# A convolution and gated-MLP kernel: a written-out order of operations rearranged between its last convolution stage and its first tile pair

## The chip, the core and the metric

The kernel runs on one NeuronCore of a Trainium2 chip. The core has five engines with a queue of instructions each, which they work off in order: TensorE (PE, matmuls), VectorE (DVE), ScalarE (ACT), GpSimd (POOL) and SyncE (SP, which here only issues DMA transfers). They meet at semaphores. PE reads SBUF and writes PSUM; the other three compute from and to SBUF, and DVE and ACT also from PSUM. The metric is the time of one execution on the device in microseconds, the median over several runs.

## The reference

Two blocks act on 2048 rows of 640 numbers, both under a modulation that is computed from a vector `c`:

```
mod = silu(c) @ w_mod                      -> sa, ca, ga, sb, cb, gb
h   = layernorm(x) * (1 + ca) + sa
kv  = shortconv4(k) * v
y   = longconv(kv, ssm_k) + kv * ssm_D     (reference: FFT over 4096)
x   = x + ga * (h * y)
h   = layernorm(x) * (1 + cb) + sb
z   = gelu(h @ w_in);  z1, z2 = halves of z
g   = w_sp @ layernorm(z2) + b_sp          (2048 x 2048 over the rows)
out = x + gb * ((z1 * g) @ w_out)
```

The long convolution is done by matrix products with trigonometric tables. The product with `w_sp` is the largest: for each pair of row tiles it takes seven block products (a Strassen-like scheme) instead of eight.

## The kernel before

The rows are 16 tiles of 128, handled in four groups of four tiles (`TB = 4`); the 640 columns are five units `u` of 128 (`NU = 5`). A first part does the convolution unit by unit; a second turns the result `xt` into `z` group by group; the third, a loop over pairs of tiles (p, p + 8) from line 1147, does the seven products and the projection with `w_out`.

The first two parts, and the first tile pair of the third, are not emitted in the order of the source. Each step is recorded with `op(...)` (line 97) as an entry of a plan: the engines that may run it, its function and what it reads and writes. The string `ORDER` (line 40) then lists all 1086 entries in the order of emission, each with the letter of the engine that runs it (P, A, D, G, S for PE, ACT, DVE, POOL, SP). Since each engine works in order, this string fixes every queue; waits follow from the data and from the buffers that are used again. There is no planner at work when the kernel is built: the order is written out by hand, or by something outside the kernel. Lines 1145 on, the main loop, are outside the plan.

The steps that are touched, with their numbers in `ORDER`:

- `res` (line 698), `xt += gh`: the residual sum of one unit of the convolution, for the four tiles of one group (512 numbers per partition) or for two (256). It may stand on DVE or GpSimd, for the last unit on DVE only. G666 to G669 are unit 2, D/G692, 697 and 702 unit 3, D728, 732, 737, 744 and 751 unit 4 (the last), 610, 611 and 644 earlier units of the later groups.
- `ghm` (line 661), two products or sums on `gh` before that (711, 712, 714), and `yml` (line 746), `gh *= y` from PSUM (D727, 731, 736, 743, 750).
- `ln2` (line 704) and `ag2` (line 829): bn_stats and bn_aggr of the new `xt`, tile by tile; `rstd2` (lines 190 and 191) on GpSimd; `nmr2` (line 833) on DVE.
- `zx` (lines 843, 845, 847): the normalised tile, on ACT, GpSimd or DVE (762, 763, 775, 776 for group 0; 840 to 843 for group 1; 906 to 909; 972 to 975).
- Group 0 comes in two pieces of two tiles. They are transposed by PE (`hfl`, line 858: P764, P765 and P777, P778) and modulated from PSUM to SBUF (`hmod`, lines 871 and 869: 766 to 770, 779 to 783). Groups 1 to 3 are transposed by a DMA (`turn`, line 889: S844, S910, S976) and modulated in place (`hmod2`, lines 897 and 895: 845 to 849, 911 to 915, 977 to 981), on DVE, ACT or GpSimd.
- `zz`: five matmuls of 432 columns for half a tile of `z1` or `z2`, 16 times for each group, each followed by `gelu` on ACT (line 920). P850, P926 and P982 or P999 are the first of groups 1, 2 and 3 that touch their group.
- `stz`, `agz`, `rstdz`, `nmrz`, `zn`: the layernorm of `z2` (lines 926, 930, 190, 935, 943 and 941).
- `ssum` (line 988, D1054 to D1061), sums of tiles of `w_sp`, and `tsum` (line 998, D1062 to D1069), sums of `z2`, for the seven products; `prodw` (line 1013, P1070 to P1083).
- `gbm` (line 1077, D1046 to D1052): `w_out` times `gb`; `bcol` D1053.
- S1038 to S1043 load `w_sp` tiles with a transposing DMA, S1045 is seven transfers of `w_out`, S1044 the bias.
- `fill`: matmuls with the identity whose result nobody uses. P1036 has four, P1037 three; both write the tile tag `s1`, of which there is one buffer, and which the first of each pair of flips also uses.

The buffers that matter: `pu` and `pz` two each and `sm` two in PSUM, `s1` one; `Z` three and `X1` four in SBUF.

Of the kernel before, what the change touches and what calls it, by code (L numbers as in the profile page):

```python
# [65 lines left out]
P425 A426 D482 D663 P664 D498 S583 P517 D518 G677 G483 G484 P485 A486 P507 D508 P499 P459 A460 P469 P501 A470 D665  # L66
G675 G519 G520 P521 A522 G509 G510 A500 A132 G708 P487 P584 D502 P513 D488 P511 A512 P491 P489 G503 A490 D514 P515
G504 D492 S678 G668 P505 P679 A516 A506 G493 D494 P495 A585 D633 D680 P681 D682 A496 P719 A720 D636 S586 P683 D684
P715 P721 A722 D716 P685 D686 D687 P717 A718 P587 A588 P723 P726 P725 G711 P724 G666 D688 D689 G714 D727 D728 D730
D759 G702 D729 P735 P749 G667 D758 D731 P1037 P589 A590 D732 D734 D691 D772 G760 D761 D762 D763 P764 D750 P765 D766  # L70
D767 D768 D733 D690 D771 P742 S756 G692 D696 D736 D737 D739 D740 A769 A770 S757 P784 A785 G773 D774 P816 A817 A776
P812 D637 D695 D836 G775 A813 P794 A795 D693 D741 D738 D834 D837 D694 D835 P777 D779 D780 D781 P778 A782 G838 D839
D840 D843 A783 P787 A788 D842 G841 D751 S844 D754 D697 D712 D743 D611 D700 D744 D748 G644 P818 P824 A825 D701 A819
D699 D746 P820 A821 P814 P805 A806 G610 D641 P791 D642 G669 D643 S1045 A815 D796 S1041 P822 A792 A823 D640 D747 D902
D848 D845 D847 P808 A809 D901 G846 P801 A849 A802 D745 D698 D706 D900 P826 D648 P798 A799 P850 D903 A851 D852 P860
A827 A861 P864 A865 P884 A885 P892 D1050 G904 D905 P867 A868 D906 D907 D909 A893 P857 P890 A858 A891 S1040 P880 A881
D793 P888 A889 G908 D803 S910 D755 P878 A879 P871 D645 G911 A913 A872 S1038 P874 P886 D866 D800 A875 P853 P882 A912
# [1133 lines left out]
```

## Time and profile before

| | |
|---|---|
| median of 3 runs | 314.68 us (314.50 to 316.01) |
| profiled execution | 314.39 us, span 312.6 us |
| PE matmuls | 298.4 us busy, 95% of the span |
| DVE | 259.9 us, 83% |
| ACT | 158.0 us, 51% |
| POOL | 117.8 us, 38% |
| granted PE clock, mean | 0.989 |

The profiled execution is one run; durations of instructions come from it, and its span begins with the first instruction and ends with the last. A row of the timeline gives the start in us from the span's beginning, the duration, engine, line, operation, what it writes and reads with shapes, the count of like instructions merged, and in brackets the idle time of the engine before it with what ended that. A row of a stretch gives, for each engine, busy time and the count of instructions, then the granted clock of PE and the share and rate of the DMA engines. Matmuls are pipelined: a row is longer than the spacing of two matmuls.

### The profile page before, as it was taken

How to read it: one execution, taken by the hardware profiler on the slowest of the kernel's cores; microseconds unless marked ns; L12 is line 12 of the kernel's file. 1: busy time of each engine (PE TensorE's matmuls, PEld its weight loads, DVE VectorE, ACT ScalarE, POOL GpSimd, SP SyncE). 2: the span in 40 equal slices, each digit the busy share in tenths (PEclk: the TensorE clock that was granted, in tenths of full speed). 3: DMA queues.
4: the chain of work that ended last, by engine and by line, in shares of the span. 5: the costliest groups of instructions: out<-in, count | busy, mean ns of one | idle time of the engine just before them, and what ended most of it. 6: DMA issues, size and time to landing. Idle time of an engine off the chain costs nothing.

```text
span 312.6 us, 6393 instructions
## 1 busy us (share of the span) xinstructions
PE 298.4 (95%) x2499; PEld 198.7 (64%) x2506; DVE 259.9 (83%) x520; ACT 158.0 (51%) x284; POOL 117.8 (38%) x147
## 2 busy tenths in 40 slices
PE   7988899999999999799799999999999999999996
PEld 2665688868899988555355555555555656555564
DVE  8898998989999998999997999977676758577473
ACT  6998899988888867166366777130101010010100
POOL 2442877858987998445315712000000000000000
PEclk9999999999999999899799999999999999999999
DMA  8999999996997679005997800065958284840414
GB/s 169 231 222 232 254 288 234 216 229 158 233 208 156 134 140 361 26 2 109 212 193 123 163 2 0 1 95 101 189 76 206 62 176 104 134 101 0 103 29 114
DMA packets 127953, 45.22 MB, mean 145 GB/s; under 512 B 117071, under 2 KB 127156, under 8 KB 127924
## 3 DMA queue, kind: packets, MB, share of 16 engines
q1 hardware_dynamic: 127770, 44.78, 67.7%
q8 instruction: 19, 0.31, 0.4%
q14 instruction: 10, 0.08, 0.1%
q10 hardware_dynamic: 154, 0.05, 0.1%
HBM read 16.11 MB, written 5.24 MB: 68 GB/s over the span
## 4 chain that ended last, share of the span: by engine, by line
PE 51%; DVE 6%; POOL 0%; issue 0%
PE ps L1013 23%; PE po L1137 10%; PE pu L245 7%; PE pz L245 7%; DVE st L704 2%; PE pz L1013 2%; PE pu L1013 1%; DVE xt L698 1%; DVE Z L847 1%; DVE gh L746 1%; DVE gh L661 0%; DVE mv L829 0%; DVE Z L871 0%; POOL rstd L191 0%; PE s L245 0%
## 5 line engine op out<-in xcount | busy, mean ns | idle before, releaser
L245 PEld LDWEIGHTS <-Z 128*128 128x128 bf16 x320 | 31.8, 100 | 30.7 <-DVE Z L897 2.7
L245 PE MATMUL pu<-X,M 128*128 128x128 bf16 (+1 forms) x480 | 45.8, 237 | 2.4 <-DVE Tf L462 2.1
L245 PEld LDWEIGHTS <-M 128*128 128x128 bf16 x480 | 37.3, 98 | 8.8 <-issue 3.3
L1019 ACT COPY m<-ps 128x432 f32<-128x432 f32 x7 | 3.6, 519 | 73.8 <-PE ps L1013 73.8
L476 POOL TENSOR_TENSOR W<-Tf 128x256 bf16<-128x256 f32 x47 | 34.7, 758 | 11.3 <-DVE Tf L462 7.9
L1013 PEld LDWEIGHTS <-S 128*128 128x128 bf16 x256 | 25.0, 98 | 21.7
L245 PE MATMUL pu<-big,Z 128*128 128x432 bf16 x160 | 33.4, 357 | 2.1 <-DVE Z L897 2.1
L248 ACT CAST X<-s 128x1024 bf16<-128x1024 f32 x31 | 31.9, 1028 | 2.0 <-PE s L245 1.8
L245 PE MATMUL pz<-big,Z 128*128 128x432 bf16 x160 | 32.7, 353 | 0.0
L1137 PE MATMUL po<-w_o,uT 128*128 128x320 bf16 (+2 forms) x231 | 32.7, 295 | 0.0
L462 DVE TENSOR_TENSOR Tf<-pu,KH 128x1024 f32<-128x1024 f32 x25 | 30.3, 1219 | 2.6 <-POOL gh L608 1.1
L1013 PEld LDWEIGHTS <-wT 128*128 128x128 bf16 x192 | 18.7, 98 | 15.5 <-issue 0.3
L1137 PEld LDWEIGHTS <-uT 128*128 128x128 bf16 (+1 forms) x231 | 22.2, 97 | 9.7
L245 PEld LDWEIGHTS <-G 128*128 128x128 bf16 x330 | 24.7, 98 | 2.3 <-issue 0.5
L248 ACT CAST KH<-pu 128x512 bf16<-128x512 f32 x40 | 23.0, 600 | 5.1 <-PE pu L245 5.1
L248 ACT CAST Z<-pz 128x512 bf16<-128x512 f32 x38 | 22.3, 601 | 5.3 <-PE pz L245 5.1
L1013 PE MATMUL ps<-X,wT 128*128 128x432 bf16 x112 | 22.7, 346 | 0.1
L1013 PE MATMUL ps<-T,S 128*128 128x432 bf16 x112 | 22.7, 346 | 0.0
L1013 PE MATMUL ps<-X,S 128*128 128x432 bf16 x112 | 21.6, 346 | 0.0
L245 PEld LDWEIGHTS <-X 128*128 128x128 bf16 x288 | 18.1, 98 | 5.1 <-DMA X<-kv_scr 1.6
L245 PE MATMUL sm<-big,dg 128*128 128x512 bf16 (+3 forms) x73 | 20.0, 382 | 0.4
L245 PE MATMUL s<-F1bd,X 128*128 128x256 bf16 x128 | 19.2, 272 | 0.5 <-ACT X L248 0.2
(181 smaller groups left out, 547.0 us busy)
## 6 DMA issues: line engine op xcount, KB each, us to landing
wm<-in_w_mod_dram SPq DMA_DIRECT2D x6, 800.0 KB, 6.1
xt<-in_A_q_dram SPq DMA_DIRECT2D x4, 640.0 KB, 6.2
out_dram<-ot SPq DMA_DIRECT2D x15, 160.0 KB, 2.1
big<-in_B_w_in_dram SPq DMA_DIRECT2D x2, 1080.0 KB, 9.6
X<-in_A_ssm_k_dram SPq DMA_DIRECT2D x4, 512.0 KB, 5.2
kv_scr<-big SPq DMA_DIRECT2D x4, 512.0 KB, 3.5
X<-kv_scr SPq DMA_DIRECT2D x4, 512.0 KB, 4.7
w_o<-in_B_w_out_dram SPq DMA_DIRECT2D x6, 160.0 KB, 2.9
```

The lines of the kernel that those rows point to most:

```text
L245: nc.tensor.matmul(o, lhsT=w, rhs=x, start=start, stop=stop)
L248: (e.copy if e is nc.scalar else e.tensor_copy)(dst, src)
L462: e.tensor_tensor(T_[:], (tl[pu] if src is None else tl[src])[:, :, :, None, :].to_broadcast(shape), tl[KH][:, :, None, :, :].to_broadcast ...
L476: e.tensor_tensor(tl[W][:, :, o, :], T_[:, :, 0, o, :], T_[:, :, 1, 1 - o, :], op=ALU.add if o else ALU.subtract)
L698: op("GD" if u < NU - 1 else "D", "res", lambda e: e.tensor_tensor(sl, sl, gl, op=ALU.add), r=[("gh", (u, g))], w=[("xt", (u, n)) for n in ...
L704: op("D", "ln2", lambda e, n=n: e.bn_stats(out=st2[:, n, (0, 0, 0, 1, 2)[u], :], in_=xt[:, n, us[0] * DU:(u + 1) * DU]), r=[("xt", (v, n)) ...
L746: op("D", "yml", lambda e, ghv=ghv, py=py, i0=i0, k=k: e.tensor_tensor(ghv, ghv, tl[py][:, i0:i0 + k], op=ALU.mult), r=[py], w=[("gh", (u, ...
L847: e.tensor_scalar(dst, xt[:, n, :], mv2[:, n, 0:1], rstd2[:, n:n + 1], op0=ALU.subtract, op1=ALU.mult)
L1013: nc.tensor.matmul(ps[:, :FC], lhsT=lhs[:, s_, :], rhs=rhs(s_), start=(s_ == 0 and not more), stop=(s_ == HT - 1), skip_group_check=more)
L1019: nc.scalar.copy(part[p, m][:], part[p, BANK[m]][:, :FC])
L1137: nc.tensor.matmul(ps[:, :hi - lo], lhsT=uTs[t][:fsz[ft], ft, :], rhs=w_o[:fsz[ft], ft, lo:hi], start=(ft == 0), stop=(ft == NFT - 1))
```

## The change

Only `ORDER` changes, from its 692nd entry on: rows 69 to 87 of the file. No step is added or dropped; what changes is the sequence, and for 33 steps the engine. Up to there every queue is as it was. The entries that changed engine: 644, 697, 702, 712 (residuals and `ghm` of units 1, 3 and 4), 762, 763, 775, 776, 840, 841, 843, 972 to 974 (`zx`), 845, 846, 848, 849, 913 to 915, 977, 979, 980 (`hmod2`), 832, 896, 897, 899, 963, 964, 1028, 1029, 1031 (`zn`). GpSimd has 29 entries in this part instead of 30, DVE 187 instead of 182, ACT 82 instead of 86.

The main moves by queue. On GpSimd: G692 comes before G760 and the residuals G667, G610 and G697 between G760 and G838; 702 and 644 go to DVE, 697 and 712 to GpSimd. On DVE: D691 comes ahead of D727, D736, D750, D737 and two `ln2` ahead of D766; D1054 to D1057 move forward to behind D810; D1060, D1061 and four of the `gbm` move behind D1084. On PE: P1036 moves from the very end to behind P1037, the `zz` of each group change places, and P1016 becomes the last. On SP: S1038 and S1039 come between S844 and S910, S1040 and S1045 between S910 and S976, the rest behind.

```diff
-P715 P721 A722 D716 P685 D686 D687 P717 A718 P587 A588 P723 P726 P725 G711 P724 G666 D688 D689 G714 D727 D728 D730
-D759 G702 D729 P735 P749 G667 D758 D731 P1037 P589 A590 D732 D734 D691 D772 G760 D761 D762 D763 P764 D750 P765 D766
-D767 D768 D733 D690 D771 P742 S756 G692 D696 D736 D737 D739 D740 A769 A770 S757 P784 A785 G773 D774 P816 A817 A776
-P812 D637 D695 D836 G775 A813 P794 A795 D693 D741 D738 D834 D837 D694 D835 P777 D779 D780 D781 P778 A782 G838 D839
-D840 D843 A783 P787 A788 D842 G841 D751 S844 D754 D697 D712 D743 D611 D700 D744 D748 G644 P818 P824 A825 D701 A819
-D699 D746 P820 A821 P814 P805 A806 G610 D641 P791 D642 G669 D643 S1045 A815 D796 S1041 P822 A792 A823 D640 D747 D902
-D848 D845 D847 P808 A809 D901 G846 P801 A849 A802 D745 D698 D706 D900 P826 D648 P798 A799 P850 D903 A851 D852 P860
...
-S976 G980 P940 A979 A941 P958 A977 P930 A931 D856 G894 D1061 A959 D929 D1055 D1057 D942 D935 P944 A945 P937 D918 A938
...
-D1068 D1069 D1078 D1082 P1074 P1076 P1083 D1075 D1079 S1080 P1010 A1011 D1084 D1048 P1018 A1019 P1022 A1023 D1049
-D1052 S1085 D1051 P1036 D1047 D1046
+P715 P721 A722 D716 P685 D686 D687 P717 A718 P587 A588 P723 P726 P725 G666 D691 G711 D689 D688 P724 D727 G714 G692
+D728 D729 D758 D730 D759 G760 D690 D731 D732 D734 P735 P1037 D772 P1036 D761 A762 P749 D736 D750 D737 P589 S756 D741
+D740 G763 P764 D766 D767 D768 S757 A590 G667 G610 D696 P765 A769 P742 D733 D738 D693 D834 D771 A770 D637 P794 G773
+D695 D836 P812 P784 A795 A813 D751 D754 D774 P818 D837 P791 A775 D739 D694 D835 G697 D698 D776 P778 G838 A819 D839
+A785 A840 D842 G843 P777 A782 A783 P787 A788 P816 A817 D780 G712 D841 P814 A815 D640 A792 D779 D781 P808 A809 D796
+D752 P822 A823 S844 P820 A821 P824 A825 A846 P798 A848 D743 D789 D702 G669 D703 D706 G845 D744 D745 D746 D900 P801
+D611 A799 D644 S1038 P805 A806 D793 P826 A802 A827 D641 D699 D901 D847 G849 P850 A851 D797 P857 P867 A868 D747 P892
+A893 D643 D701 D755 D748 P882 D903 S1039 A883 D700 D642 D902 A858 P874 A875 D647 P880 G904 D905 D906 G908 D786 D907
+D909 S910 D810 A881 P890 A891 P860 G915 A861 P864 A865 G911 P871 A872 P884 D1054 D1055 D1057 D705 D968 A912 D1056 D807
+D811 G913 A885 D648 D704 D753 D645 D966 D646 D967 D969 G970 D866 P888 A889 S1040 D859 D862 D863 P886 A914 P878 A887
+A879 P853 D790 D971 D972 G975 D973 A974 A854 D855 D800 P926 P916 A927 S1045 P937 A917 D852 D869 S976 D1046 D803 D804
...
+D964 D1064 D1066 D1030 A1028 A1015 D1029 D1065 P1024 P1070 A1025 P1072 S1044 P1077 D1067 P1081 D1053 A1073 D1068 D1069
+A1071 P1074 D1078 D1082 P1076 D1075 D1079 S1080 P1083 P1018 A1019 P1022 P1010 A1023 D1084 S1085 A1011 D1060 D1061
+P1016 A1017 D1047 D1051 D1052 D1050
```

More of the change, by code (lines that the diff above doesn't have):

```diff
@@ L73 @@
-D840 D843 A783 P787 A788 D842 G841 D751 S844 D754 D697 D712 D743 D611 D700 D744 D748 G644 P818 P824 A825 D701 A819
-D699 D746 P820 A821 P814 P805 A806 G610 D641 P791 D642 G669 D643 S1045 A815 D796 S1041 P822 A792 A823 D640 D747 D902
-D848 D845 D847 P808 A809 D901 G846 P801 A849 A802 D745 D698 D706 D900 P826 D648 P798 A799 P850 D903 A851 D852 P860
-A827 A861 P864 A865 P884 A885 P892 D1050 G904 D905 P867 A868 D906 D907 D909 A893 P857 P890 A858 A891 S1040 P880 A881
-D793 P888 A889 G908 D803 S910 D755 P878 A879 P871 D645 G911 A913 A872 S1038 P874 P886 D866 D800 A875 P853 P882 A912
@@ L78 @@
-A887 A854 D705 A883 D869 D647 D968 D752 D704 D810 D753 D646 D967 D969 D703 D966 D1060 D914 D1058 G970 D971 D915 A972
-G973 D859 D804 P926 P916 A917 D1059 G975 D807 A927 D811 D789 P948 D876 S1044 D1053 P952 S1039 D1056 D928 D873 D877
-A949 P923 A924 G974 D870 P946 A947 A953 D855 P919 A920 D786 D790 D925 D797 P954 D1054 A955 D862 D863 G828 P933 A934
-S976 G980 P940 A979 A941 P958 A977 P930 A931 D856 G894 D1061 A959 D929 D1055 D1057 D942 D935 P944 A945 P937 D918 A938
-D895 D898 A899 D897 D896 G978 D921 D922 D829 D832 G981 D939 D943 P999 D932 D936 G960 P982 A1000 D830 A983 D984 S1042
@@ L83 @@
-D1001 P992 A993 P1020 A1021 D961 P989 A990 D1063 D833 P985 A986 P1006 A1007 A962 P996 A997 D965 P1003 A1004 D831 P1024
-D994 D991 D995 D987 D988 P1014 D1008 P956 D1005 D1009 A1025 A1015 P1016 D998 D1002 G1026 D963 D1062 A964 D1064 D1027
-D1030 A957 A1017 P1012 A1013 S1043 P950 A1029 A951 P1072 A1073 D1028 P1070 D1031 D1065 A1071 D1066 D1067 P1077 P1081
-D1068 D1069 D1078 D1082 P1074 P1076 P1083 D1075 D1079 S1080 P1010 A1011 D1084 D1048 P1018 A1019 P1022 A1023 D1049
-D1052 S1085 D1051 P1036 D1047 D1046
+P715 P721 A722 D716 P685 D686 D687 P717 A718 P587 A588 P723 P726 P725 G666 D691 G711 D689 D688 P724 D727 G714 G692
@@ new lines @@
+P933 D918 S1041 A934 P930 P940 A938 D1048 A941 D876 D873 D877 D870 D856 D928 A931 D932 D980 P919 D942 A920 G894 P923
+D921 A924 P948 P958 G979 P952 D895 A959 D922 A949 P946 P954 D977 A896 D925 D929 A947 A953 A955 D939 G978 G981 P982
+A983 G828 P999 D1058 D1059 A897 D898 A1000 D943 P985 A986 P989 A990 P992 D829 D830 D831 D1049 A832 D833 D935 D936
+D1001 D984 D987 A993 D988 P944 P1006 A945 A1007 P996 A997 D1062 P1003 A1004 D991 P956 G960 D961 D965 A962 A957 D1008
+D998 D1002 D1005 D1009 P1020 S1043 A1021 A963 S1042 D994 D995 D899 D1063 P1012 P1014 A1013 P950 G1026 D1027 A1031 A951
```

## The prediction

> **What bounds the kernel now.** I read the page's engine shares (PE 95%, DVE 83%), then the chain that ended last, then busy time by stretches cut at PE's gaps, then the timelines of PE, DVE and POOL around them. The chain, in order of time (start, us, what):
>
> ```profile
> 139.41 1.56 DVE Z L847 x3
> 140.97 1.30 DVE xt L698
> 142.59 0.97 DVE xt L698
> 149.93 0.68 DVE Z L897 x2
> 206.53 0.88 PE s L245 x4
> 207.45 8.92 PE ps L1013 x48
> ```
>
> Up to 150.6 the chain runs on VectorE; from 150.66 it is matmul after matmul to the end. Two VectorE handoffs and then pure PE work set the time. Stretches (PE, PEld, DVE, ACT, POOL busy, then granted clock):
>
> ```profile
> 128.27:130.47 2.20, 0.00 (x0) 0.00 (x1) 2.13 (x7) 0.43 (x1) 1.77 (x2) 1.00 0.00 0
> 130.47:134.19 3.72, 3.63 (x48) 2.59 (x49) 3.41 (x10) 1.02 (x2) 0.53 (x2) 0.54 0.02 4
> 148.60:150.66 2.06, 0.00 (x1) 0.01 (x1) 2.03 (x8) 0.53 (x1) 0.00 (x0) 1.00 0.87 255
> 150.66:155.09 4.43, 4.43 (x16) 2.00 (x16) 3.91 (x14) 1.48 (x3) 2.19 (x3) 0.61 0.98 204
> 155.09:207.45 52.36, 52.31 (x286) 27.89 (x285) 49.05 (x114) 31.45 (x57) 15.26 (x18) 1.00 0.46 82
> ```
>
> PE stands still twice, and each time runs at about half clock for 3 to 4 us afterwards. Then it has no idle left. Timelines of VectorE and GpSimd (start, us, shape, count):
>
> ```profile
> 128.06 0.29 DVE L698 TENSOR_TENSOR xt<-xt,gh 128x256 bf16<-128x256 bf16 x1
> 129.19 0.87 DVE L833 SCALAR_TENSOR_TENSOR nmr<-mv,rstd 128x2 f32<-128x2 f32 x1
> 140.89 1.36 DVE L698 TENSOR_TENSOR xt<-xt,gh 128x512 bf16<-128x512 bf16 x1
> 142.50 1.05 DVE L698 TENSOR_TENSOR xt<-xt,gh 128x512 bf16<-128x512 bf16 x1
> 145.48 0.42 DVE L698 TENSOR_TENSOR xt<-xt,gh 128x512 bf16<-128x512 bf16 x1
> ```
>
> ```profile
> 128.90 1.14 POOL L698 TENSOR_TENSOR xt<-xt,gh 128x512 bf16<-128x512 bf16 x1
> 140.76 3.80 POOL L698 TENSOR_TENSOR xt<-xt,gh 128x512 bf16<-128x512 bf16 x3
> ```
>
> The same residual takes 0.42 alone and 1.36 beside a GpSimd one; nmr2 (0.14 alone, row 135.25) takes 0.87 and ends at 130.06, with GpSimd's 130.04.
>
> **The Trainium skill.** "SBUF — State Buffer", Who interferes with whom: the port pair that VectorE and GpSimd share is an exclusive lock; a VectorE operation with two SBUF inputs, or in a two-port mode, and a GpSimd operation that reads SBUF block each other, whoever comes second. The trace agrees (0.42 against 1.36). "TensorE: Matmul & The Clock Gate", What's actually happening: the array's clock is halved after an idle window of some 3.4 us, in free-running windows. The half clock and its length agree (3.72 and 4.43 us stretches); that a whole idle window is needed does not: 2.06 us sufficed here, while 1.06 us (PE's timeline at 22.4) left the clock at 1.00.
>
> **The loss before.** Running groups overlap by 0.16 in the timeline, so the gaps cost 2.20 + 0.16 = 2.36 and 2.06 + 0.16 = 2.22. Slow clock: from 130.47 to 134.19, 10 transposes (0.055 each at full rate, from the pair at 136.93), 32 short matmuls (0.80) and 5 long ones (0.91) would take 2.26; they took 3.72: 1.46. From 150.66 to 155.09, 15 long ones at 0.182: 2.73 instead of 4.43: 1.70. Sum 7.74 us. PE's other work from 128 to the main loop is the same in both kernels, the fillers too, so what counts is how much of 7.74 remains.
>
> **The change, part by part** (letter and number are ORDER's).
>
> *Fillers P1036.* Four matmuls (0.216 apart, 0.86) leave the end, where they are on the chain, and go behind P1037. They run in the first gap. They write the one s1 buffer that P1037 writes, so a drain of about 0.2 comes in between (a row is 0.38 long, 0.216 apart). PE's last group before the gap starts at 127.43, five times 0.136 apart, so PE is free at 128.11 + 0.86 + 0.2 = 129.2.
>
> *First handoff.* One more bn_stats goes ahead of D727, which had waited for PE until 125.36: +0.1. Residual D728 now finds GpSimd free (only G692 is left there, over by 125.3): 0.29 instead of 0.90. The second ag2 then ends at 127.74 + 0.1 − 0.6 = 127.24. rstd2 takes 0.1 + 1.07 (row 127.84): 128.4. Five VectorE operations (1.62, as 127.66 to 129.28) run until 128.8, nmr2 unblocked until 128.95. The two normalisations go to ACT (0.91) and GpSimd (0.88) at once and end at 129.9; before, both stood on VectorE until 130.77 and PE started at 130.47. PE starts at 129.95: idle 0.75.
>
> *First matmuls of group 0.* Ten transposes and P742: 0.55 + 0.80, PE free at 131.3. VectorE does D736 and D750 (0.66 each, one input in PSUM: no lock) until 130.1; residual D737 then meets G667, which starts at 129.85 and takes 1.15: blocked, it ends 0.28 after it, as in the 140.89 row: 131.3. Two bn_stats (0.2 apart), then the hmods: first at 132.15, next two 0.33 apart. Idle 0.85, and 0.3 inside the first group: 1.15.
>
> *Second piece.* Five groups of 0.91 bring PE to 137.0. The flips need tiles 2 and 3. VectorE's statistics in front (six operations from 132.75, 0.2 to 0.4 each) end with D771 at 134.25; rstd2 0.95: 135.2. G697 then takes the port (1.15 + 0.15 behind D751), so nmr2 D774 ends at 136.55 (the old collision, in a new place, 0.65). A775: 137.5. D776, behind five statistics (1.3): 138.2. Idle 1.2. Third and fourth tiles' hmods are done at 141.3 (D841 blocked 0.3 by G843), when PE wants them at 138.75 + 3 × 0.91 = 141.5.
>
> *Second handoff.* Normalised tiles of group 1 are ready at 140.35, the transposing DMA issues at 140.4 (before 141.06) and lands after 5.75 as before (ACT's wait for it ended at 146.85): 146.15. The five hmod2 were two on ACT/POOL and three on VectorE behind its bn_stats, until 150.93. Now two on POOL (2 × 0.77), two on ACT (2 × 0.81), one on VectorE: 148.0. PE arrives at 141.5 + 8 × 0.91 = 148.8. No gap, margin 0.8; so the second slow stretch goes as well.
>
> *Afterwards.* SP's queue holds turn, wT 0, wT 8, turn, wT 1, seven w_o, turn. Group 2's turn issues at 153.8, lands 5.7 to 6.7 later (range of the three turns before), POOL's three hmod2: 162 to 163; PE needs them after 16 groups, 163.4. The w_o issues (3.5, rows 146.65 to 150.15) and wT 1 leave SP by 163.0; group 3's tiles are ready at 164.6, landing 170.4, POOL again three: 174.4; PE wants them 13 groups after 163.4: 175.2. Last T2 sum: before 196.0 for a matmul at 196.33; with everything 4 to 5 earlier the same 0.3 to 0.5 stays. The four sums and w_o products moved behind D1084 (2 × 0.64, 4 × 0.40) end about 203.4, and are first needed about 208.6 (S) and 211.5 (w_o).
>
> **Sum.** Remaining: 0.2 + 0.75 + 1.15 + 1.2 = 3.3; for the margins of 0.2 to 0.8, which hang on landings known only to 1 us, I add 0.5: 3.8. Saved 7.74 − 3.8 = 3.9. Against the profiled execution (314.39, span 312.6): 310.5; the median shown is 0.3 above it: 310.8. I take 310.6. Its own range, 309.4 to 311.6: from no slip at the margins (0.5 less) and half of the 1.2 wait gone, to 1 us more of slips.
>
> **Rivals.**
> - *Waits move on (0.20).* The hmods of the second piece stand behind two lockable operations with a margin of 0.2; a landing of 6.7 costs another 0.4 to 1. Together 1.5 on top: 312.1 (311.6 to 313.1). For: seven VectorE operations were blocked between 120 and 200 for 4.1 us in all, and D737, D774, D841 will be. Against: ACT has idle time there. That the change doesn't do what it says, since GpSimd residuals still stand beside lockable operations, is this case.
> - *No gain (0.11).* If the second piece's wait reaches 2 us, the clock halves again (1.7): 3.9 − 2 − 1.7 = 0.2 left: 314.5. The two early idles (0.75, 0.85) within 3 us sum to 1.6, between 1.06 that left the clock alone and 2.06 that didn't; but those 1.5 would mostly be absorbed by the 1.2 wait for the flips.
> - *Slower (0.06).* D1054 to D1057 now stand in VectorE's queue at 154.2, ahead of group 3's statistics, waiting for wT 0 and wT 8. The second issues at about 146.2 and lands 4.5 to 5.8 later (range of the wT rows): 152. If it lands after 159, VectorE stalls 5 us, group 3's matmuls come 4 later (5 less 0.8 margin) and the clock drops (1.7): 310.6 + 5.7 = 316.3. Below 159 it isn't slower.
> - *More gain (0.03).* Below 309.4: margins hold and overlap more.
>
> **Numbers.** 0.5% is about what a measurement here can tell: 313.1 and 316.3 are the bounds. Faster: 0.60 + 0.20 + 0.03 = 0.83; same 0.11; slower 0.06. The range, 309.3 to 313.0, leaves out the last three cases, 0.20 together.
>
> **What would show it.** Right: first matmul of the main loop near 203.5 instead of 207.45; gaps of PE about 0.8, 0.9, 0.6, 0.6 between 129 and 139, none near 148.6; granted clock 1.00 from 129 to 155; nmr2 of the first piece 0.14. Wrong: a clock below 0.9 there, a PE gap over 1 us before group 1, 2 or 3, or DVE waiting for a DMA at D1054.

## The result, and the profile after

The changed kernel took 312.04 us (median of 4, 310.68 to 312.31) beside 315.35 us of the kernel before (median of 4, 314.50 to 316.26): ratio 0.9886, interval 0.9841 to 0.9931. On a second chip the medians were 310.90 us (4 executions) beside 313.81 us (16): ratio 0.9904, interval 0.9874 to 0.9935. The ratios here and below are of mean times, without the few executions that took over 1.5% longer than the fastest of their kernel. So it is 1.0 to 1.1% faster; the medians lie 3.3 and 2.9 us apart. The forecast was 310.6 us, in a range from 309.3 to 313.0.

One thing in the section on the change stands the wrong way round: in the changed part VectorE has 182 entries after the change and 187 before it, ScalarE 86 and 82, GpSimd 30 and 29. Work goes from VectorE to the other two, as the prediction takes it.

The profiled execution of the changed kernel took 312.19 us, with a span of 310.4 us. It has to be aligned before the two profiles can be compared. VectorE's wait for the load of a block of the convolution kernel, far ahead of the changed part and in both kernels alike, was 1.05 us in the profile of before and 2.03 here, and from there on everything is 1.4 us later. I therefore measure **the stretch**: from the first matmuls of the last shared convolution step, P724, to the first matmul of the main loop. It was 207.45 − 124.97 = 82.48 us before and 205.26 − 126.40 = 78.86 us after, that is 3.62 us less. A second profile of the changed kernel gave 204.18 − 126.05 = 78.13.

The chain that ended last, after, in order of time (start, us, what):

```profile
...
155.21 6.38 DMA Z<-Z
161.83 2.27 POOL Z L897 x3
164.46 1.02 POOL rstd L191
...
193.94 1.07 DVE T L998
195.05 0.89 PE pu L1013 x4
...
205.43 8.76 PE ps L1013 x48
```

Before, the chain was matmul after matmul from 150.66 on. Now it runs through VectorE, a transposing DMA and GpSimd up to the last T2 sum at 193.94, and only from 195.05 on is it matmuls alone. TensorE itself has no gap from 150.08 to 191.85, so VectorE's queue is close behind it there and decides only at the end. The stretches at TensorE's gaps (PE, PEld, DVE, ACT, POOL busy, then the granted clock):

```profile
130.78:131.27 0.49, 0.00 (x1) 0.01 (x1) 0.49 (x2) 0.49 (x2) 0.49 (x2) 1.00 0.00 0
132.82:133.59 0.77, 0.00 (x1) 0.01 (x1) 0.77 (x4) 0.32 (x1) 0.77 (x1) 1.00 0.11 21
138.59:139.71 1.12, 0.57 (x8) 0.43 (x8) 0.73 (x3) 1.00 (x3) 0.84 (x2) 1.00 0.00 0
150.08:191.85 41.77, 41.77 (x229) 22.31 (x228) 35.67 (x93) 28.87 (x53) 15.04 (x20) 1.00 0.62 120
191.85:195.05 3.20, 2.36 (x14) 1.17 (x13) 3.10 (x6) 1.96 (x4) 0.00 (x0) 1.00 0.00 0
```

The two gaps of 2.2 and 2.06 us are gone, the clock is 1.00 throughout, and there is no wait at all before group 1 (its first matmul is at 150.08, less 1.43 for the later start 148.65). What is left are small waits between 130.8 and 139.7, and a new one between 191.85 and 195.05. The timelines of VectorE and GpSimd that answer to those of before:

```profile
127.40 0.29 DVE L698 TENSOR_TENSOR xt<-xt,gh 128x256 bf16<-128x256 bf16 x1
130.15 0.10 DVE L833 SCALAR_TENSOR_TENSOR nmr<-mv,rstd 128x2 f32<-128x2 f32 x1
131.36 1.34 DVE L698 TENSOR_TENSOR xt<-xt,gh 128x512 bf16<-128x512 bf16 x1
136.98 0.83 DVE L833 SCALAR_TENSOR_TENSOR nmr<-mv,rstd 128x2 f32<-128x2 f32 x1
```

```profile
131.27 2.44 POOL L698 TENSOR_TENSOR xt<-xt,gh 128x512 bf16<-128x512 bf16 x2
136.63 1.15 POOL L698 TENSOR_TENSOR xt<-xt,gh 128x512 bf16<-128x512 bf16 x1
```

The first piece's nmr2 is free (0.10 instead of 0.87). But the change has not taken all residuals on GpSimd from beside VectorE's SBUF operations: D737 takes 1.34 instead of 0.42 next to G667, and the second piece's nmr2 0.83 next to G697.

### The profile page after: what moved, and what is told of

It is laid out like the page before. It is cut to its first block, busy times and chain, and to the rows that moved or that the text cites. A ratio compares the mean times of both kernels' runs of the same rounds, so it can differ in the third digit from the quotient of the medians.

```text
span 310.4 us, 6397 instructions
## 1 busy us (share of the span) xinstructions
PE 295.9 (95%) x2499; PEld 197.3 (64%) x2506; DVE 254.1 (82%) x515; ACT 160.9 (52%) x288; POOL 116.0 (37%) x148
## 4 chain that ended last, share of the span: by engine, by line
PE 37%; DVE 19%; POOL 2%; DMA 2%; issue 1%; ACT 1%; POOLq 1%; DVEq 0%; SPq 0%
PE ps L1013 23%; PE po L1137 10%; DVE stz L926 4%; DVE st L704 3%; DMA Z<-Z 2%; PE pz L1013 1%; DVE Tf L462 1%; PE pu L245 1%; DVE xt L698 1%; DVE X L943 1%; POOL rstd L191 1%; DVE T L998 1%; DVE T L462 1%; DVE mv L829 1%; DVE gh L746 1%
## 5 line engine op out<-in xcount | busy, mean ns | idle before, releaser
L245 PE MATMUL pu<-big,Z 128*128 128x432 bf16 x160 | 32.5, 346 | 0.0
```

Source lines behind the costliest of these rows:

```text
L245: nc.tensor.matmul(o, lhsT=w, rhs=x, start=start, stop=stop)
```

## The experiments

Each kernel was measured beside the kernel before on the same chip. The table gives the stretch, from one profile of each, and the ratio of mean times, from 4 to 20 executions of each. A wait of TensorE is a bracket of the timeline plus the 0.16 by which running groups overlap. The intervals of the changed kernel and of all the kernels below it in the table, but for the undone second handoff, overlap: times alone don't put these in order.

| kernel | stretch, us | ratio to before | interval |
|---|---|---|---|
| before, first and second profile | 82.48, 81.59 | | |
| before, fillers alone | 79.72 | 0.9979 | 0.9955 to 1.0003 |
| before, second handoff alone | 80.53 | 0.9970 | 0.9947 to 0.9993 |
| before, one GpSimd residual alone | 81.42 | 0.9985 | 0.9960 to 1.0009 |
| before, nine fillers in the second gap | 79.95 | 0.9963 | 0.9940 to 0.9987 |
| changed, first and second profile | 78.86, 78.13 | 0.9886, 0.9904 | 0.9841 to 0.9931, 0.9874 to 0.9935 |
| changed, second handoff undone | 81.64 | 0.9988 | 0.9960 to 1.0015 |
| changed, last steps reordered | 78.34 | 0.9910 | 0.9875 to 0.9945 |
| changed, rstd2 of group 3 first | 78.13 | 0.9883 | 0.9862 to 0.9905 |
| changed, second piece reordered | 77.25 | 0.9896 | 0.9868 to 0.9923 |
| the same and the last steps | 76.71 | 0.9868 | 0.9829 to 0.9907 |
| the same and a load moved | 76.65 | 0.9870 | 0.9830 to 0.9910 |

My theory from the prediction: the loss is in two handoffs, which the lock lengthens, and in the slow clock that follows when TensorE stands idle. The rivals: the fillers alone do it by keeping TensorE warm; the clock has another cause; the gap only moves on.

### The fillers alone

```diff
-D759 G702 D729 P735 P749 G667 D758 D731 P1037 P589 A590 D732 D734 D691 D772 G760 D761 D762 D763 P764 D750 P765 D766
+D759 G702 D729 P735 P749 G667 D758 D731 P1037 P1036 P589 A590 D732 D734 D691 D772 G760 D761 D762 D763 P764 D750 P765 D766
...
-D1052 S1085 D1051 P1036 D1047 D1046
+D1052 S1085 D1051 D1047 D1046
```

> The kernel before with one edit: the four filler matmuls go from the end of the stage into the first gap of TensorE. The stretch from the last shared convolution matmuls (at 124.97 before) to the first matmul of the main loop was 82.48 us before, 78.86 in the changed kernel. Theory A (two handoffs, the second fixed by VectorE and the transposing DMA): the gap near 129 shrinks to about 1.0, TensorE keeps its full clock after it, but group 1 is ready no earlier, so the gap near 148 grows from 2.06 to about 3.3 and the half clock after it stays; saved 1.1 (the 0.9 that left the end, and 0.2), stretch 81.4, time 0.3% less. Rival B (the fillers are the gain: TensorE kept warm early): saved 2.3 (0.9 and the slow clock's 1.46), stretch 80.1, time 0.7% less.

The stretch was 79.72, that is 2.76 less than in the first profile of before. In the timeline of TensorE (start, us, shape, count, idle before):

```profile
131.17 0.81 PE L858 MATMUL s<-ident,Z 128*128 128x128 bf16 x6 [1.11 <-DVE Z L847]
151.08 1.09 PE L245 MATMUL pu<-big,Z 128*128 128x432 bf16 x5 [1.23 <-DVE Z L897]
```

Group 1 began 25.39 after P724, before 25.69: as theory A says, that handoff is fixed by others. But the rest came out otherwise. After an idle of only 1.11 us the clock was at half again (fifteen long matmuls took 4.42 instead of 2.73 us), and because TensorE was slowed there it arrived late at the second gap, which was 1.23 instead of 3.3, and the clock stayed full behind it. Over all executions the gain was 0.2%, hardly to be told from none. So rival B's 0.7% falls, and theory A had the cost of the fillers right and the clock wrong: one profile doesn't show what the clock does on the average. Of rival B something stays: by their mean clocks (how they are read is said with the second profile of before) 7 of the 20 executions had no slow stretch, against 1 of 71 of the kernel before on this chip, and these 7 took 1.5 us less than the 12 with one.

### The second handoff alone

```diff
-D699 D746 P820 A821 P814 P805 A806 G610 D641 P791 D642 G669 D643 S1045 A815 D796 S1041 P822 A792 A823 D640 D747 D902
-D848 D845 D847 P808 A809 D901 G846 P801 A849 A802 D745 D698 D706 D900 P826 D648 P798 A799 P850 D903 A851 D852 P860
+D699 D746 P820 A821 P814 P805 A806 G610 D641 P791 D847 D642 G669 D643 S1045 A815 D796 S1041 P822 A792 A823 D640 D747 D902
+G845 P808 A809 D901 G846 P801 A849 A848 A802 D745 D698 D706 D900 P826 D648 P798 A799 P850 D903 A851 D852 P860
```

> The kernel before with the second handoff alone changed: of group 1's five modulation steps one goes from VectorE to ScalarE, one from VectorE to GpSimd, and the one left on VectorE goes up its queue. Theory A: the gap near 148.6 falls from 2.06 to 0.3 or less, the granted clock after it is 1.00, the first gap and its half clock stay; saved 3.4 (2.22 + 1.70 less 0.5), stretch 79.1, time 1.1% less: alone nearly as much as the whole change. Rival B (the gap moves on, since group 2's tiles or the last T2 sum aren't ready 3.4 us sooner): a gap over 1 us further back, saved less than 2, stretch over 80.5.

The gap before group 1 and the half clock behind it are gone as theory A says, and yet the stretch shrank by 1.95, not 3.4. TensorE's timeline further back has two new waits:

```profile
163.77 0.36 PE L245 MATMUL pz<-big,Z 128*128 128x432 bf16 x1 [0.45 <-DVE Z L897]
177.23 0.36 PE L245 MATMUL pz<-big,Z 128*128 128x432 bf16 x1 [0.27 <-POOL Z L897]
```

These are groups 2 and 3, whose tiles weren't ready 3.4 us sooner. They account for about one us of the missing 1.5; the rest I can't place to a single wait. Rival B holds in part: alone, the second handoff is worth 0.3% (0.05 to 0.5).

### One residual off the first handoff

```diff
-D759 G702 D729 P735 P749 G667 D758 D731 P1037 P589 A590 D732 D734 D691 D772 G760 D761 D762 D763 P764 D750 P765 D766
-D767 D768 D733 D690 D771 P742 S756 G692 D696 D736 D737 D739 D740 A769 A770 S757 P784 A785 G773 D774 P816 A817 A776
+D759 G702 D729 P735 P749 G667 D758 D731 P1037 P589 A590 D732 D734 D691 D772 G692 G760 D761 D762 D763 P764 D750 P765 D766
+D767 D768 D733 D690 D771 P742 S756 D696 D736 D737 D739 D740 A769 A770 S757 P784 A785 G773 D774 P816 A817 A776
```

> The kernel before with one edit: the GpSimd residual that blocked the first piece's nmr2 goes ahead of rstd2, before the values that rstd2 needs are there. Theory A (exclusive lock): nmr2 takes 0.14 instead of 0.87, TensorE's gap near 129 is 0.5 shorter (1.6 to 1.7), and the half clock after it stays; saved 0.5 at most, because group 1's handoff at 148.6 swallows what VectorE doesn't gain; stretch 82.0 to 82.5. Rival B (nmr2's 0.87 was a wait for something else than GpSimd's residual): nmr2 stays over 0.8, stretch 82.5.

VectorE's timeline has "129.10 0.10 DVE L833" for the first piece's nmr2. With the GpSimd residual alone moved away, 0.87 became 0.10: the lock is shown for this place, as "SBUF — State Buffer" in the Trainium skill has it (Who interferes with whom). TensorE's gap fell to 1.41 + 0.16. This time the clock stayed at 1.00 behind it, TensorE came earlier to group 1, waited 2.48 us there, and half clock followed after that. In time it is worth nothing that can be told from zero (0.15%, interval −0.1 to 0.4%): freed work ahead of a handoff that others fix turns into idle.

### Nine fillers in the second gap

```diff
-FILLS = (4, 6, 2, 2, 4, 3, )
+FILLS = (4, 6, 2, 2, 9, 3, )
...
-D848 D845 D847 P808 A809 D901 G846 P801 A849 A802 D745 D698 D706 D900 P826 D648 P798 A799 P850 D903 A851 D852 P860
+D848 D845 D847 P808 A809 D901 G846 P801 A849 A802 D745 D698 D706 D900 P826 D648 P798 A799 P1036 P850 D903 A851 D852 P860
...
-D1052 S1085 D1051 P1036 D1047 D1046
+D1052 S1085 D1051 D1047 D1046
```

> The kernel before with matmuls added: the last fillers go into the second gap of TensorE, ahead of group 1's first matmul, and are nine instead of four (1.94 us in a gap of 2.06; five more matmuls than before in all). Nothing else moves. Theory A (the clock halves because TensorE stood idle): group 1 still starts at about 150.66, the clock is 1.00 after it, saved 1.70 and the 0.88 that left the end: 2.6, stretch 79.9, time 0.8% less with more work. Rival B (the clock was lowered for another cause, such as the DMA traffic or the load of this stage): clock 0.6 as before from 150.7 to 155, saved 0.9, stretch 81.6.

Busy times and clock, first after the untouched first gap, then after the filled one:

```profile
130.13:136.22 6.09, 5.96 (x58) 3.38 (x58) 5.94 (x20) 2.28 (x5) 1.78 (x3) 0.72 0.01 3
150.58:156.06 5.48, 5.48 (x32) 2.93 (x31) 5.03 (x16) 2.50 (x5) 2.41 (x3) 1.00 0.91 199
```

Behind the filled gap the clock was 1.00 with the DMA engines nearly as busy as before (0.91 against 0.98), so in this execution neither that traffic nor the stage's load halved it. That the fillers kept it up is not shown: the second profile of before, below, had the full clock behind the same gap without them, and 2 of the 20 executions here still had two slow stretches (9 of 71 before). The stretch was 2.53 shorter than in the first profile of before; 2.6 was expected. In time the edit gained 0.4% and not 0.8%: 1.2 us, interval 0.4 to 1.9. The 0.88 us of the four fillers that left the end is in that, so five more matmuls in a wait cost nothing that could be seen, and what they gain through the clock can't be told from nothing.

### The kernel before and the changed one again

> The kernel before once more, for a second profile of it. Theory A: the number of slow-clock stretches differs from execution to execution while the two gaps of TensorE (2.36 and about 2.2 us) stay. With both (mean clock 0.989) the stretch to the main loop is 82.5; with the one after the first gap alone (0.995) 80.8; with the one after the second gap alone TensorE arrives earlier, waits about 3.5 before group 1 and the stretch is 82.5 again. Rival B: both slow stretches are in each execution of this kernel, clock 0.989.

In the second profile of before TensorE had gaps of 2.19 and 1.94 us, as in the first, but only one slow stretch (granted clock after the two gaps):

```profile
130.17:135.80 5.63, 5.50 (x57) 3.62 (x58) 5.22 (x17) 2.24 (x5) 1.44 (x3) 0.70 0.01 3
150.35:155.00 4.65, 4.65 (x26) 2.50 (x27) 4.16 (x14) 2.51 (x5) 2.41 (x3) 1.00 0.91 210
```

The stretch was 81.59 (80.8 expected; part of the difference is a wait of 0.27 + 0.16 before group 3 that the first profile didn't have). Each execution has its mean granted clock with its time. A slow stretch costs 1.5 to 1.7 us, some 0.005 of that mean, so 0.989 stands for two of them and 0.993 to 0.995 for one. Of 127 executions of the kernel before, 17 had two, 108 one and 2 none. The profile that I predicted from was the rarer kind. It was hardly a slower kind, though: each taken against the mean of its chip, the 17 took 0.3 us longer than the 108, with an error of about 0.2. A slow stretch behind the first gap is partly paid back, since TensorE then waits less before group 1 (1.23 us with it where the fillers moved alone, 2.48 without it where one residual moved alone). Which gap the one slow stretch of the 108 followed can't be read from a mean.

> The changed kernel as it is, beside as many executions of the kernel before as the single parts had (the first comparison had four of each). Theory A (TensorE's idle is gone for good, so its clock stays at 1.00 in every execution): clock 0.999 to 1.00 throughout, stretch to the main loop 78.9 us, and 2 to 2.5 us less than the kernel before, of which most executions here had a mean clock of 0.995, that is one slow stretch and not the two that were profiled. Rival B (the 1.1% of the first comparison): 3.3 us less.

2.9 us less in the medians, between the two theories; the interval (2.0 to 4.0 us) holds both. Of the changed kernel's 8 executions 7 had a clock of 0.999 or 1.00 and one 0.994, and of the 20 of the kernel below in which only rstd2 of group 3 moves, 16, with three at 0.994 and one at 0.989. Before, 2 of 127 were without a slow stretch: they have become rare, but not impossible.

### The second handoff undone

```diff
-D752 P822 A823 S844 P820 A821 P824 A825 A846 P798 A848 D743 D789 D702 G669 D703 D706 G845 D744 D745 D746 D900 P801
+D752 P822 A823 S844 P820 A821 P824 A825 A846 P798 D743 D789 D702 G669 D703 D706 D848 D845 D744 D745 D746 D900 P801
```

> The changed kernel with the second handoff undone: the two modulation steps that went to ScalarE and GpSimd are on VectorE again, at the place in its queue that they have in the changed kernel. Theory A: they end 1.5 to 2 later, TensorE waits 1.5 to 2 us before group 1 (no wait in the changed kernel), and whether its clock halves after that (1.7 more) depends on the execution; stretch 80.5 to 82.4 against 78.86, time 0.5 to 1.1% above the changed kernel. Rival B (VectorE has room for both by then): stretch within 0.5 of 78.86.

TensorE waited 1.43 + 0.16 before group 1, and the stretch was 81.64. In the median 2.4 us of the 2.9 to be had on this chip are gone again (313.29 against 310.90, and 313.81 before). So the second handoff is needed for the whole, though alone it gave 0.3%. The clock is no part of this loss: 9 of the 12 executions kept it full. Later waits for ScalarE of 0.35 and 0.48, at 166 and 170, make up most of the rest of the stretch. VectorE shows why: at this place in its queue it waits 1.86 us for the transposing DMA before the two steps, and further back, as in the kernel before, it reached them only at 149.93, behind the statistics. Part of the 2.4 is that wait, which neither of the two kernels has, so the number is an upper bound for what the two engines' letters are worth.

### The last steps reordered

```diff
-D998 D1002 D1005 D1009 P1020 S1043 A1021 A963 S1042 D994 D995 D899 D1063 P1012 P1014 A1013 P950 G1026 D1027 A1031 A951
-D964 D1064 D1066 D1030 A1028 A1015 D1029 D1065 P1024 P1070 A1025 P1072 S1044 P1077 D1067 P1081 D1053 A1073 D1068 D1069
+D998 D1002 D1005 D1009 P1020 S1043 A1021 A963 S1042 D994 D995 D899 D1063 P1012 P1014 A1013 P950 G1026 D964 D1027 A951 A1031
+D1030 A1015 D1029 D1028 D1064 D1065 D1066 P1024 P1070 A1025 P1072 S1044 P1077 D1067 P1081 D1053 A1073 D1068 D1069
```

> The changed kernel with its last steps reordered: behind the last group's rstdz VectorE does the three normalisations it needs and the T2 sums first and the sum into the first tile afterwards, one more normalisation comes from ScalarE to VectorE, and ScalarE drains one matmul group ahead of its normalisation. Theory A (the changed kernel lost 0.33 + 0.84 = 1.17 us of its gain at 192 to 195 because the order of VectorE's queue behind rstdz put the last T2 sum 4.84 us after it, against 2.88 in the kernel before): both waits of TensorE go, stretch 77.7, time 0.35% under the changed kernel. Rival B (VectorE is full to the end there, so another order only moves the wait): a wait of over 0.5 stays, stretch over 78.4.

Both waits were gone: the second half of the T2 product follows the first without a gap. The stretch was 78.34, not 77.7, because in this execution the clock was at half after the small waits at 130 to 133 (0.64 from 132.85 to 137.56), which cost 1.61, of which the waits for the flips (0.90) and inside the first group (0.28) were absorbed; 78.86 − 1.17 − 1.18 + 1.61 is 78.12, and 0.22 remains. The time did not tell it from the changed kernel (311.14, five executions, against 310.90). What the lines show is the order: VectorE in the changed kernel, behind rstdz,

```profile
190.19 0.16 DVE L935 SCALAR_TENSOR_TENSOR nmrz<-mvz,rstdz 128x4 f32<-128x4 f32 x1 [0.90 <-POOL rstdz L191]
190.27 0.50 DVE L943 TENSOR_SCALAR X<-X,mvz,rstdz 128x864 bf16<-128x864 bf16 x1
190.97 1.06 DVE L998 TENSOR_TENSOR T<-X,T 128x1728 bf16<-128x1728 bf16 x1 [0.20 <-DVE X L943]
191.95 1.05 DVE L998 TENSOR_TENSOR X<-X,X 128x1728 bf16<-128x1728 bf16 x1
192.92 0.91 DVE L943 TENSOR_SCALAR X<-X,mvz,rstdz 128x864 bf16<-128x864 bf16 x2
193.94 1.06 DVE L998 TENSOR_TENSOR T<-X,T 128x1728 bf16<-128x1728 bf16 x1
```

in the kernel before,

```profile
193.43 0.15 DVE L935 SCALAR_TENSOR_TENSOR nmrz<-mvz,rstdz 128x4 f32<-128x4 f32 x1
193.51 1.33 DVE L943 TENSOR_SCALAR X<-X,mvz,rstdz 128x864 bf16<-128x864 bf16 x3
194.94 1.06 DVE L998 TENSOR_TENSOR T<-X,T 128x1728 bf16<-128x1728 bf16 x1
```

and with the reordered steps:

```profile
189.43 1.33 DVE L943 TENSOR_SCALAR X<-X,mvz,rstdz 128x864 bf16<-128x864 bf16 x3
190.67 2.02 DVE L998 TENSOR_TENSOR T<-X,T 128x1728 bf16<-128x1728 bf16 x2
```

From the end of rstdz to the end of the last T2 sum it is 195.00 − 190.15 = 4.85 in the changed kernel, 196.00 − 193.12 = 2.88 before, and 192.69 − 189.31 = 3.38 here. In the changed kernel a normalisation and two sums stand in between that the last T2 sum doesn't need.

### rstd2 of group 3 first

```diff
-D909 S910 D810 A881 P890 A891 P860 G915 A861 P864 A865 G911 P871 A872 P884 D1054 D1055 D1057 D705 D968 A912 D1056 D807
-D811 G913 A885 D648 D704 D753 D645 D966 D646 D967 D969 G970 D866 P888 A889 S1040 D859 D862 D863 P886 A914 P878 A887
+D909 S910 D810 A881 P890 A891 P860 A861 P864 A865 P871 A872 P884 D1054 D1055 D1057 D705 D968 A912 D1056 D807
+D811 A885 D648 D704 D753 D645 D966 D646 D967 D969 D911 D913 G970 G915 D866 P888 A889 S1040 D859 D862 D863 P886 A914 P878 A887
```

> The changed kernel with one edit in the middle: GpSimd does rstd2 of group 3 ahead of group 2's modulation steps, of which two go to VectorE (where they stand ahead of the wait for that rstd2) and one stays on GpSimd behind it. The last steps are left as they are. Between the two profiles of the changed kernel the landing of group 2's transposing DMA differed by 0.9 us (6.4 and 5.5), and the wait of VectorE for rstd2 behind it was 2.54 and 1.64, the wait for the last T2 sum 1.17 and 0.43. Theory A (a landing that TensorE doesn't wait for reaches it by way of VectorE's queue: GpSimd's rstd2 stands behind three steps that wait for the DMA, VectorE waits for that rstd2, and everything to the T2 sums comes later): the wait of VectorE falls to 0.6 or less plus what the two steps wait for the DMA themselves, the T2 wait is gone or under 0.2, stretch to the main loop 77.6 to 77.9 (78.86 and 78.13 before this edit), time 0.1 to 0.4% under the changed kernel. Rival B (only the order of VectorE's queue behind rstdz sets the last T2 sum): VectorE's wait falls, but a T2 wait of 0.4 or more stays, stretch 78.1 or more.

VectorE and TensorE, the waits that are left:

```profile
165.88 2.14 DVE L926 BATCH_NORM_STATS2 stz<-X 128x6 f32<-128x432 bf16 x4 [1.41 <-ACT X L920]
194.43 0.89 PE L1013 MATMUL pu<-T,S 128*128 128x432 bf16 x4 [0.26 <-DVE T L998]
```

The wait for rstd2 is gone, as theory A says; in its place VectorE waits 1.41 us for ScalarE's drained matmuls, that is for TensorE. The T2 wait is 0.26 + 0.16, just as in the second profile of the changed kernel, and so is the stretch, 78.13. Rival B wins: 0.42 is what the order behind rstdz costs even when VectorE is in time. The 0.73 between the two profiles of the changed kernel fits the landing of group 2's transposing DMA, 0.9 later in the first. That it reached TensorE by this way is argued from the two timelines (a wait for rstd2 of 2.54 against 1.64), and no run set it by itself.

### The second piece reordered, and a faster kernel

```diff
-D728 D729 D758 D730 D759 G760 D690 D731 D732 D734 P735 P1037 D772 P1036 D761 A762 P749 D736 D750 D737 P589 S756 D741
-D740 G763 P764 D766 D767 D768 S757 A590 G667 G610 D696 P765 A769 P742 D733 D738 D693 D834 D771 A770 D637 P794 G773
-D695 D836 P812 P784 A795 A813 D751 D754 D774 P818 D837 P791 A775 D739 D694 D835 G697 D698 D776 P778 G838 A819 D839
-A785 A840 D842 G843 P777 A782 A783 P787 A788 P816 A817 D780 G712 D841 P814 A815 D640 A792 D779 D781 P808 A809 D796
-D752 P822 A823 S844 P820 A821 P824 A825 A846 P798 A848 D743 D789 D702 G669 D703 D706 G845 D744 D745 D746 D900 P801
-D611 A799 D644 S1038 P805 A806 D793 P826 A802 A827 D641 D699 D901 D847 G849 P850 A851 D797 P857 P867 A868 D747 P892
+D728 D729 D758 D730 D759 G760 D690 D731 D732 D734 P735 P1037 D772 P1036 D761 A762 G763 P749 D736 D733 D771 G773 D737 P589 S756
+P764 D766 D767 D774 G776 G667 G610 D768 D750 D741 D637 D738 D740 S757 A590 D696 P765 A769 P742 D693 D834 A770 A775 P794
+D695 D836 P812 P784 A795 A813 D751 D754 P818 D837 P791 D739 D694 D835 P778 P777 D780 D779 D781 G838 A819 D839
+A785 A782 A783 A840 D842 G843 P787 A788 P816 A817 G712 G697 D841 P814 A815 D640 A792 P808 A809 D796
+D752 P822 A823 S844 P820 A821 P824 A825 A846 P798 A848 D743 D702 G669 D703 D698 D706 G845 D744 D745 D746 D900 P801
+D611 A799 D644 S1038 P805 A806 P826 A802 A827 D641 D699 D901 D847 G849 P850 A851 P857 P867 A868 D747 P892
...
-D909 S910 D810 A881 P890 A891 P860 G915 A861 P864 A865 G911 P871 A872 P884 D1054 D1055 D1057 D705 D968 A912 D1056 D807
+D909 D789 D793 D797 S910 D810 A881 P890 A891 P860 G915 A861 P864 A865 G911 P871 A872 P884 D1054 D1055 D1057 D705 D968 A912 D1056 D807
```

> The changed kernel with the collisions of its second piece taken out: the residual D737 goes ahead of the copy D750 and of the three modulation steps, rstd2 of the second piece goes ahead of GpSimd's residuals G667 and G610, the residual G697 goes behind group 1's normalisation, the second piece's normalisations and modulation steps follow earlier, and three bn_stats of group 0 go behind group 2's normalisations. The last steps are left as they are. Theory A (the waits of 0.91 and 0.28 ahead of and in the first group, and of 0.39 and 0.52 at the flips are what the lock still costs; behind them VectorE has less slack): 2.1 of waiting goes, 0.5 to 0.9 of it comes back before group 1, and the wait for the last T2 sum stays; stretch to the main loop 77.3 to 77.9 (78.13 and 78.86 in the two profiles of the changed kernel), nmr2 0.10 to 0.16 in both pieces. Rival B (VectorE's queue sets the T2 sums, so everything gained ahead is waited for there): stretch 78.1 to 78.9, with a wait of 1.5 or more at 190 to 195.

The collisions were gone: nmr2 took 0.10 and 0.15, the residual D737 0.36. TensorE waited nowhere between 132.91 and 142.62, then 0.38 and, before group 1, 0.93 (for ScalarE to drain an earlier group of matmuls, which stands in its queue behind two modulation steps that wait 1.87 us for the transposing DMA), and 0.42 for T2. The edit also gives the second normalisation of this piece (776) to GpSimd. The stretch was 77.25, a little under theory A's span. All 14 executions had the full clock.

With the last steps reordered as well, and three VectorE operations put behind D1084:

```diff
-A983 G828 P999 D1058 D1059 A897 D898 A1000 D943 P985 A986 P989 A990 P992 D829 D830 D831 D1049 A832 D833 D935 D936
+A983 G828 P999 A897 D898 A1000 D943 P985 A986 P989 A990 P992 D829 D830 D831 A832 D833 D935 D936
...
-D998 D1002 D1005 D1009 P1020 S1043 A1021 A963 S1042 D994 D995 D899 D1063 P1012 P1014 A1013 P950 G1026 D1027 A1031 A951
-D964 D1064 D1066 D1030 A1028 A1015 D1029 D1065 P1024 P1070 A1025 P1072 S1044 P1077 D1067 P1081 D1053 A1073 D1068 D1069
-A1071 P1074 D1078 D1082 P1076 D1075 D1079 S1080 P1083 P1018 A1019 P1022 P1010 A1023 D1084 S1085 A1011 D1060 D1061
-P1016 A1017 D1047 D1051 D1052 D1050
+D998 D1002 D1005 D1009 P1020 S1043 A1021 A963 S1042 D994 D995 D899 D1063 P1012 P1014 A1013 P950 G1026 D964 D1027 A951 A1031
+D1030 A1015 D1029 D1028 D1064 D1065 D1066 P1024 P1070 A1025 P1072 S1044 P1077 D1067 P1081 D1053 A1073 D1068 D1069
+A1071 P1074 D1078 D1082 P1076 D1075 D1079 S1080 P1083 P1018 A1019 P1022 P1010 A1023 D1084 S1085 A1011 D1058 D1059 D1060 D1061
+P1016 A1017 D1047 D1051 D1052 D1050 D1049
```

> The kernel of the run above with the last steps reordered as in the run on the last steps, and with three VectorE operations that nothing needs so soon (two products for the second S sum and one for w_o, 1.74 us together) moved from ahead of the T2 sums to behind the first half of the stage's results. Theory A: no wait over 0.3 from 160 to the main loop, stretch 76.6 to 77.1, time 1.4 to 1.6% under the kernel before. Rival B (the order of the tail is not what limits it): stretch as in the run above.

The stretch was 76.71, no wait over 0.1 is left from 165 to the main loop, and the time 308.70 us beside 313.45: 1.3% faster than the kernel before, interval 0.9 to 1.7%. It was taken beside before, not beside the changed kernel; by the stretches it is 1.4 to 2.1 us ahead of that, and the times don't show it, since the intervals overlap.

One load moved in the shared part, on the same kernel:

```diff
-A328 P321 A322 D591 P267 A268 G288 P329 A330 S575 G547 D548 S70 P295 D296 D297 P578 D579 A274 P576 G561 D577 D562 D594
-P313 A557 A314 P309 P331 A332 P61 D652 S94 D96 G298 D563 D564 G655 A310 P67 D62 P311 P375 D68 A312 P349 D350 P333 D334
+A328 P321 A322 D591 P267 A268 G288 P329 A330 S575 G547 D548 S94 S70 P295 D296 D297 P578 D579 A274 P576 G561 D577 D562 D594
+P313 A557 A314 P309 P331 A332 P61 D652 D96 G298 D563 D564 G655 A310 P67 D62 P311 P375 D68 A312 P349 D350 P333 D334
```

> The same with one load moved in a part that all these kernels share: the load of the fourth block of the convolution kernel, for which VectorE waited 0.7 to 2.2 us near 67 in most profiles, issues ahead of the transposing load of 4.2 to 5.7 us that stood before it on the queue. Theory A (it was late only because of that place): the wait is gone, the last shared convolution matmuls come 1 us earlier and vary less from execution to execution, time 0.3% under the run above. Rival B (the transposing load is as urgent, or the buffer isn't free): no change, or a wait of the same size at the next transposed block.

VectorE no longer waited at that place (0.48 us in the run before this one, 2.31 in the one before that), the stretch was 76.64, and the last shared convolution step began at 123.96 (124.77 and 128.04 in the two runs beside it). The median, 308.68 of 4, doesn't show it: theory A stands on the profile only.

## Why the prediction was right, step by step

Put in the prediction's own terms, with a wait counted from the starts of the matmuls (the start of the one that waited, less where the usual spacing would have put it; this is bracket plus 0.16 to within 0.03), the first profile of the changed kernel and the second:

| step | forecast | first | second |
|---|---|---|---|
| fillers' drain | 0.2 | 0.21 | 0.21 |
| first handoff | 0.75 | 0.65 | 0.66 |
| first matmuls of group 0 | 1.15 | 0.91 + 0.28 | 0.90 + 0.29 |
| second piece (flips) | 1.2 | 0.38 + 0.52 | 0.39 + 0.52 |
| second handoff | 0 | 0 | 0 |
| slow clock | 0 | 0 | 0 |
| ScalarE's drain, last T2 sum | within the 0.5 for margins | 0.33 + 0.84 | 0 + 0.43 |
| sum | 3.8 | 4.12 | 3.40 |

7.74 − 4.12 is 3.62 and 7.74 − 3.40 is 4.34, and these are the differences of the stretches (3.62 and 4.35): the ledger closes. The forecast of 3.9 lies between. Two small terms are in neither sum and nearly cancel: the drain of the fillers was there before too (their last one starts at 207.02, the main loop 0.43 later, where 0.22 is the usual spacing), so it is moved and not new; and a pause of 0.16 at 142.4 is new.

**What held.** The two handoffs and the half clock were the loss, and most of it went. The first matmul of the main loop stands at 203.83 when aligned (near 203.5 forecast). First handoff and first matmuls came within 0.1 each, with D737 blocked by G667 to within 0.1 of where the step put it (1.34). The second piece had its nmr2 blocked by G697, as said, and lost 0.90 instead of 1.2. The second handoff had no gap: its last modulation step ended 147.53 (aligned; 148.0 forecast) and TensorE arrived at 148.65 (148.8). The "Slower" rival fell: D1054 began without a wait at 155.08. "No gain" fell as well, with the clock at 1.00; that is what 7 of 8 executions did, and the bound that it set between 1.06 and 2.06 us of idle is not what the clock goes by (last section). Of "Waits move on" the blocked operations came as described, but what they cost was within the sum.

**What was mis-sized.** "Afterwards", last T2 sum: "with everything 4 to 5 earlier the same 0.3 to 0.5 stays". It doesn't. The step moved the sum along with everything else and didn't go through VectorE's queue behind rstdz, where the change puts three more operations in front of it (4.85 against 2.88 us). It also took the wrong need for the margin: the last T2 sum is read by the second half of its product, at 197.06 (196.33 and four matmuls of 0.182), so the margin before was 1.06 and not 0.33. In the profile with the last steps reordered the wait is gone. It cost 0.43 to 0.84 us; the other 0.33 of the first profile was a wait for ScalarE (`0.17 <-ACT G L920`).

**What was luck.** Too much was charged at the flips (0.3) and at the first handoff (0.1), and the 0.5 for margins was set aside for the landings before groups 2 and 3, where no wait came. These paid for the T2 wait that the sum didn't have.

**What was right for too simple a reason.** The slow clock was counted at 1.46 + 1.70 from one profile and at nothing after. The second is right for 7 of 8 executions, the first for 17 of 127: mostly there is one slow stretch. By the second profile of before the stretch to beat was 81.59, 0.9 less; in the times two slow stretches cost only 0.3 us more than one, so how much smaller the usual saving is stays open. The medians say 2.9 to 3.3 us and not 3.9, with intervals wide enough to hold 3.9. From 310.6 to the measured 312.04 it is 0.7 for a median of before that was higher than the one shown when I predicted, and the rest for the smaller saving. The parts needn't add up either: alone, the fillers, the second handoff and one freed residual gave 0.2, 0.3 and 0.15%, and the whole 1.0 to 1.1%. Their intervals leave room for a sum of 1%, and they are not the whole change: that the first piece's normalisations now run on ScalarE and GpSimd at once, no run tried by itself.

## What to carry to other kernels

Removing one wait is worth only as much as the next handoff leaves of it: go through the queue of the engine that makes the next input, up to the instruction that the waiting one really reads, before you write that "the same margin stays". Read the mean clock of many executions, not the slow stretches of one profile, before counting on their removal. Where TensorE must wait anyway, matmuls that do nothing can cost no time at all.

## What the runs showed of the hardware

**The clock after an idle.** Idle of TensorE, and the granted clock behind it, in the profiles of this case: 2.20 us, 2.19, 2.20 and 2.19 were followed by half clock each time; 2.06 by half, 1.94 by full; 2.48 by half; 1.43, 1.41 and 1.23 by full; 1.11 by half; 0.49 and 0.77 within 2.8 us by full in four profiles and by half in one. The half clock began 0.06 to 1.9 us after the matmuls had begun again. So the length of the idle doesn't decide it. The clock that the traces hold shows what goes with it. A window of before and the one after it, then one of its second profile and one of the last steps reordered (the first and the last were followed by half clock, the third by full):

```profile
147.60:151.01 3.41, 1.35 (x8) 0.46 (x7) 3.38 (x13) 1.01 (x3) 0.11 (x1) 1.00 0.86 251
151.01:154.42 3.41, 3.41 (x12) 1.54 (x11) 2.89 (x12) 1.20 (x3) 1.52 (x3) 0.50 1.02 201
```

```profile
147.53:150.94 3.41, 1.47 (x9) 0.59 (x8) 3.38 (x13) 0.82 (x2) 0.00 (x0) 1.00 0.92 271
```

```profile
130.14:133.55 3.41, 2.25 (x45) 1.71 (x46) 3.38 (x8) 1.67 (x4) 2.83 (x3) 1.00 0.02 5
```

Every stretch of half clock between two busy parts lasts 3.41 us, and within one execution they begin whole multiples of 3.41 us apart: 130.53 and 151.01 are six, and in the second profile of before 130.47 and 311.37 (at the kernel's end) are 53. So a trace with one slow stretch shows where its windows lie. What goes with it is the work in the window ahead. As an estimate, I count each matmul by its columns at the spacing of the long ones (432 columns in 0.182 us). Then the eight windows ahead of these half clocks in the 14 profiles are filled to 0.24 to 0.36, and none of the other 1170 or so with full clock to less than 0.37. The windows of before are at 0.32 and 0.34. The one at 147.53 in its second profile is at 0.38 and keeps the full clock; the one at 130.14 looks busier, but 32 of its matmuls have 16 columns, and it is at 0.34. This is read from the traces and fits all of them; no run set the filling by itself, and the bound between 0.36 and 0.37 is no better than the estimate. By this, an idle of 2 us costs the clock where it falls mostly into one window and need not where it is split between two, and very short matmuls beside it hardly help. "TensorE: Matmul & The Clock Gate" of the Trainium skill (What's actually happening) says that the windows run free of the kernel, which fits; that the whole window must be idle is contradicted by these numbers.

**GpSimd's last power.** The second instruction of the last rstdz (line 191, a power, by which GpSimd makes the inverse root) took 1.70 us in both profiles of before and 1.82 in each of the changed one, against 1.01 for the same shape at the three other places. It is the last instruction that GpSimd computes; the profile names GpSimd's own sequencer and no cause. It stood on the chain that ended last.

**A load that comes when it likes.** Between 0 and 2.3 us of wait for the same load went with a start of the last shared convolution step anywhere from 123.82 to 128.04 us in profiles of kernels that are the same up to there. It is not all of the spread: the latest had another wait for a load of 0.84 at 45.55, and with the same wait of 0.8 the start was 124.90, 126.05 or 126.50.
